# Attention block with a query tile's two passes run together at the start: key tiles in turn, two open banks of sums

## The chip, the cores and the metric

One core of a Trainium2 chip runs the whole kernel. The metric is device time in microseconds (us) of one execution. Five engines work side by side, each through its own list of instructions in order: TensorE (PE, matrix products), VectorE (DVE), ScalarE (ACT, here above all the exponentials), GpSimd (POOL) and SyncE (SP, which issues the DMAs). An instruction that has to wait holds up all that stands behind it on its engine. Matrix products land in PSUM, eight banks of 128 x 512 fp32.

## What is computed

A transformer block over 2048 tokens of width 640: layer norm, attention with 32 heads of 20 that share one key and one value head, residual; then layer norm, a gated GELU feed-forward of width 1536, residual.

```
q = (ln(x) @ wq)  as 32 heads of 20;   k = ln(x) @ wk;   v = ln(x) @ wv
p = softmax(q k^T / sqrt(20));   h = x + (p v, heads joined) @ wo
out = h + (gelu(ln(h) @ w_gate) * (ln(h) @ w_up)) @ w_down
```

The large part is the softmax: 32 x 2048 x 2048 exponentials.

## The kernel before

**Blocks, quads, passes.** The queries are cut into 16 tiles of 128 tokens, the keys too. A *pass* `(t, h)` is half `h` (16 heads, as 4 groups of 4) of query tile `t`: 32 passes in all. A *unit* or block is 128 keys x 512 (4 heads x 128 queries); the four blocks `hl` of a key tile in a pass make a *quad*. A pass has 16 quads, 64 blocks.

**Two ways to an exponential.** Most blocks go to ScalarE: `qk` (L873) writes scores to a bank, the exponential (L973) writes probabilities to `pbuf`, and PE multiplies by `v_ext` (L1087). ScalarE's blocks come in *cycles* of five: three blocks in banks 0 to 2 (an instruction of 128x1536) and two in banks 3 and 4 (128x1024). The last few key tiles of each pass go to VectorE instead (`stream_d`): it makes the exponential from the bits of an integer (L927, one instruction a block) and two shifted copies (L938, two a quad), which PE adds with weights `v_w`. `D_QUADS` gives the number of such key tiles by pass, `D_AHEAD` and `D_BEFORE_END` the cycles among which they are spread, and where `D_IN_SET` is 1 some cycles (places 1, 2, 4 and 6 of a pass) keep two blocks in the first set and leave its third bank to VectorE.

**Banks.** 0 to 2 and 3 to 4 hold scores. Bank 6 (`PVB`, `PV_pool`) holds the open sum of a pass, one pass at a time. Banks 5 and 7 (`AUX_pool`, `aux()`) are the side banks: projections, PE transposes, feed-forward, and the blocks for VectorE.

**Order.** Every engine's order is made ahead of the run by a planner (`_Sched`). Tasks carry dependences, priorities, an expected duration and slots of pools; it plays through them and writes the engines' lists with the semaphore waits. PE has three sources: the stream of score groups in fixed order (`sc.stream`), each with a margin (`spare`, from `MARGIN` and `MARGIN_2`); the sums (`Units`), which take as many finished quads as fit; and the rest. `PATIENCE`, `LAG` and `URGENT` are digits by pass or tile that shift these choices. The chip itself only sees the lists.

**The start.** SP loads x and the first half of wq (L578). Token tile by token tile, VectorE and GpSimd do the layer norm (L621 to L644), the tile is transposed (tile 0, and those in `T_CUT`, by PE, L667; the others by a DMA, L653), PE projects k and v (`kv_proj`, L701 and L703), and VectorE evicts them to `kT4` and `v_ext` (L712, L717). `q_first` projects the first half of query tile 0's q, enough for pass (0,0). The second half of wq is loaded once tile 9 is normalised, and `q_half(0, 1, ...)` with its DMA transpose `q_dma` (L747) makes the second half of q after that, for pass (0,1):

```
units += [(t, h, kt, hl) for kt in range(NT - n) for hl in range(4)]
if t == 9:
    dma_wq.append(load("sp", wq_sb[:, :, D // 2:D], ..., "wq1", 4.0, [ln1_nm[t]]))
...
q_half(0, 1, tk0, after_=[ln1_nm[Q_AFTER[0]]])
q_dma(0, tk0, 4)
```

**The rest.** When the last block of a pass is placed, `pv_open` opens its sum. When the sum is closed, `normalise` transposes it (L1106), divides and passes it on (L1113); then come `wo_proj`, a layer norm and `ffn`, interleaved with the next passes. The last tile is done by `last_tile` once the exponentials are over.

Of the kernel before, what the change touches and what calls it, by code (L numbers as in the profile page):

```python
# [45 lines left out]
class _Sched:  # L46
# [7 lines left out]

    PATIENCE = "42444444444444444442444443444444"
    WINDOW, ACTIVE, GAP = 3.42, 1.45, 0.25
# [48 lines left out]
    def schedule(self):  # L105
# [120 lines left out]
        while left:  # L226
            best = None
# [73 lines left out]
            if isinstance(t, int):  # L301
                t = self.units.take(at, t)
                for s in t.acq:
                    s.index = min(s.pool.open_for(s))
                    s.pool.busy[s.index] = True
                    t.extra += s.pool.users[s.index]
                    s.pool.users[s.index] = []
            else:
                ready[e] = [c for c in ready[e] if c[1] is not t]
                for s in t.acq:  # L310
                    p = s.pool
                    i = min(p.open_for(s), key=lambda i: (p.free_at[i], i))
# [105 lines left out]
def bass_sequential_preLN__grouped_kv_mqa__glu_gated_geglu__prompt_kernel(  # L418
# [93 lines left out]
    def bank(b):  # L512
        return ps[:, b * 512:(b + 1) * 512]
# [46 lines left out]

    LAG = "5333333333335533"
    T_CUT = {1: 5}
    KV_POOL = ()
# [20 lines left out]
    x_ready[2] = x_ready[3] = load("sp", xh[:, 2:4, :], x_view[:, 2:4, :], "x2", 4.9)  # L584
    dma_wq = [load("sp", wq_sb[:, :, 0:D // 2], wq_view[:, :, 0:D // 2], "wq0", 6.3)]
    for a in (4, 8):
        d = load("sp", xh[:, a:a + 4, :], x_view[:, a:a + 4, :], f"x{a}", 4.2 + a if a == 4 else 10.2)
        for t in range(a, a + 4):
            x_ready[t] = d
# [218 lines left out]
    def d_units(t, h):  # L808
        return 4 * int(D_QUADS[2 * t + h])

    D_QUADS = "04454544444444445444444444453533"
    D_AHEAD = "32222222222225222222222124223222"
    D_BEFORE_END = "33333333333333233331334233343233"
    MARGIN = "03333333233335333112333220613330"
    MARGIN_2 = "56666666666666366662666666343662"
    D_IN_SET = "11111111111111111111111111111111"

# [3 lines left out]
    units, d_kts, quads = [], {}, {}  # L821
    for t, h in passes:
        n = d_units(t, h) // 4
        quads[(t, h)] = [(len(units) + 4 * kt, kt) for kt in range(NT - n)]
        units += [(t, h, kt, hl) for kt in range(NT - n) for hl in range(4)]
        d_kts[(t, h)] = list(range(NT - n, NT))
    INSET = (1, 2, 4, 6)
# [16 lines left out]
    for p in passes:  # L844
        left = 4 * d_kts[p]
        if not left:
            continue
        for n in in_set:
            if cycles[n][0][0][:2] == p:
                d_of[(n, 2)] = p  # L850
                left = left[:-1]
        i = passes.index(p)
        n0, n1 = max(0, in_pass[p][0] - int(D_AHEAD[i])), in_pass[p][-1] - int(D_BEFORE_END[i])
        own = [(n, 1) for n in range(n0, n1 + 1) if (n, 1) not in d_of and len(cycles[n][1]) == 2]
        more = len(left) - len(own)
# [88 lines left out]
    def stream(n):  # L944
# [38 lines left out]
        for p in passes:  # L983
            if n == in_pass[p][-1]:
                pv_open(p)
# [14 lines left out]
    def pv_open(p):  # L1000

        t, h = p
        sl = state["pv"] = PV_pool.slot()
        for u, kt in quads[p]:
# [7 lines left out]
        end.opens = False  # L1012
        pending.append((p, sl, end))
        normalise(t, h, sl, end)

    class Units:


        def __init__(self):
            self.begun = False  # L1020

        def lists(self):
            p, sl, end = pending[0]
            return p, sl, end, owed[p], d_terms[p]

        @staticmethod
        def when(deps):
            return max(d.end + sc.HOP[d.eng] if d.end is not None else 1e9 for d in deps)

        def look(self, now):  # L1030

            if not pending:
                return None, 0
            p, sl, end, mine, terms = self.lists()
            base = 0.0
            if not self.begun:
                if sl.pool.busy[0]:
                    return None, 0
                base = sl.pool.free_at[0]
            at = [max(base, self.when(x[0])) for x in mine[:12]] + [max(base, self.when(x[0])) for x in terms]  # L1040
            at = [x for x in at if x < 1e8]
            if not at:
                return None, 0
            return min(at), sum(x <= now + 0.02 for x in at)

        def urgent(self):
            p, sl, end, mine, terms = self.lists()
            n = len([x for x in mine[:12] if self.when(x[0]) < 1e8])
            return n >= int(URGENT[sc.phase]) or p == passes[-1] or not any(
                x for x in mine if self.when(x[0]) > 1e8)  # L1050

        def take(self, now, n):
            p, sl, end, mine, terms = self.lists()
            got = []
# [6 lines left out]
            assert got  # L1061
            first = not self.begun
            last = not mine and not terms and not d_owed[p]
            t = end if last else sc.add("pe", None, 0.0, [], name=f"pv_{p}", cfg="col")
            t.deps = [d for x in got for d in x[0]]
            if first:
                t.acq = [sl]
                t.opens = lambda: bank(PVB)
            if last:
                t.opens = False  # L1070
                pending.pop(0)
            self.begun = not last
            for x in got:
# [4 lines left out]
            def fn(e):  # L1078
                ins = None
                for i, x in enumerate(got):  # L1080
# [17 lines left out]

    def normalise(t, h, pv_sl, pv_t):
# [325 lines left out]
    q_evicted[(0, 2)] = ln1_nm[Q_AFTER[1]]  # L1425
# [194 lines left out]
```

## Time and profile before

| | |
|---|---|
| time, median of 3 runs | 767.12 us (766.24 to 769.23) |
| the profiled execution's own time | 767.44 us |
| its span, first to last instruction | 765.8 us |
| PE busy | 722.0 us (94%) |
| DVE busy | 687.4 us (90%) |
| ACT busy | 732.5 us (96%) |
| L973, the exponentials on ACT | 667 instructions, 706.4 us |
| first exponential starts | 10.16 us |
| mean granted TensorE clock | 0.993 |

How to read it: the span is cut from one execution of the program; 1.6 us of that execution's time lie outside it. "Busy" is the time in which an engine ran at least one instruction. A line such as L973 is the line of the kernel before; in the changed kernel the same statements stand some lines lower. Rows of a timeline give the start, the length of the merged piece, the engine, the line, output <- input, the count, and in brackets the idle time ahead of it with what ended it.

### The profile page before, as it was taken

To read this page: it belongs to the slowest core of one execution; us is meant where nothing else is said; L and a number is where in the kernel's file an instruction comes from. 1 tells how busy PE (TensorE), PEld (TensorE's weight loads), DVE (VectorE), ACT (ScalarE), POOL (GpSimd) and SP (SyncE) were. 2 spreads that over 40 slices of the span, in tenths; PEclk is the share of its full clock that TensorE was granted. 3 is DMA by queue.
4 is the path that set the end of the run, shared out by engine and by line. 5 is a ranking of instruction groups with operands and counts; after the bars stand their busy time and mean duration, and the time that the engine had idled before them with its cause. 6 is when DMAs were issued, how large, how long until landed. Compare 5 with 4: busy or idle time off the path is not lost.

```text
span 765.8 us, 23888 instructions
## 1 busy us (share of the span) xinstructions
PE 722.0 (94%) x10693; PEld 264.3 (35%) x10693; DVE 687.4 (90%) x1275; ACT 732.5 (96%) x702; POOL 111.7 (15%) x185
## 2 busy tenths in 40 slices
PE   7898899999999999999999999999999999999987
PEld 3432233333333333333233333333333332333346
DVE  7777999999999999888999999999999999899862
ACT  5899999999999999999999999999999999999961
POOL 5410112001011111111101011021102101112100
PEclk9899999999999999999999999999999999999999
DMA  6692001020200303020001202102101200201201
GB/s 169 144 358 46 1 19 24 2 45 20 45 19 13 43 10 45 20 45 19 10 16 39 45 20 45 19 11 43 34 19 24 45 20 1 40 10 31 43 11 42
DMA packets 80604, 31.66 MB, mean 41 GB/s; under 512 B 71536, under 2 KB 79216, under 8 KB 80496
## 3 DMA queue, kind: packets, MB, share of 16 engines
q1 hardware_dynamic: 79184, 30.03, 18.1%
q8 instruction: 85, 1.39, 0.8%
q10 hardware_dynamic: 1312, 0.05, 0.1%
q14 instruction: 23, 0.19, 0.1%
HBM read 10.21 MB, written 2.62 MB: 17 GB/s over the span
## 4 chain that ended last, share of the span: by engine, by line
ACT 81%; PE 14%; DVE 3%; DMA 1%; issue 0%; SPq 0%; POOL 0%
ACT pbuf L973 78%; PE ps L533 5%; PE ps L873 4%; PE ps L1087 3%; ACT g_z L1241 2%; PE ps L1356 1%; DVE dbuf L927 1%; DMA wq_sb<-in_A_wq_dram 1%; DMA xnT<-xn_tmp 0%; PE ps L1365 0%; DVE g_gs L1226 0%; PE ps L701 0%; DVE stats L623 0%; SPq L578 0%; DVE stats L621 0%
## 5 line engine op out<-in xcount | busy, mean ns | idle before, releaser
L973 ACT ACTIVATE pbuf<-ps 128x1024 bf16<-128x1024 f32 (+1 forms) x667 | 706.4, 1267 | 5.1 <-PE ps L873 4.7
L927 DVE TENSOR_SCALAR dbuf<-ps 128x512 int16<-128x512 f32 x504 | 333.4, 684 | 33.2 <-PE ps L873 30.0
L873 PE MATMUL ps<-qT,kT 32*128 32x512 bf16 x2048 | 285.7, 386 | 27.3 <-ACT pbuf L973 21.8
L938 DVE TENSOR_SCALAR dbuf<-dbuf 128x2048 int16<-128x2048 int16 x252 | 168.4, 689 | 0.9
L873 PEld LDWEIGHTS ps<-qT,kT 32*128 32x128 bf16 x2048 | 74.0, 91 | 270.3 <-ACT pbuf L973 225.1
L1087 PE MATMUL ps<-pbuf,v_ext 128*32 128x512 bf16 (+3 forms) x2084 | 147.2, 331 | 0.6 <-ACT pbuf L973 0.4
L1087 PE MATMUL ps<-dbuf,v_w 128*32 128x512 bf16 x1512 | 132.2, 382 | 2.0 <-DVE dbuf L938 1.2
L1228 POOL TENSOR_TENSOR g_z<-g_gs 128x512 bf16<-128x512 bf16 x45 | 51.0, 1133 | 271.8 <-DVE g_gs L1226 271.8
L533 PE MATMUL ps<-wu_sb,xnT 128*32 128x512 bf16 x900 | 68.1, 383 | 1.8 <-DVE g_gs L1226 1.0
L1087 PEld LDWEIGHTS ps<-pbuf,v_ext 128*32 128x32 bf16 x2084 | 44.6, 94 | 67.9 <-issue 49.9
L533 PE MATMUL ps<-wd_sb,hhT 128*32 128x320 bf16 x1440 | 67.0, 301 | 0.0
L533 PE MATMUL ps<-wg_sb,xnT 128*32 128x512 bf16 x900 | 66.8, 382 | 0.1
L1087 PEld LDWEIGHTS ps<-dbuf,v_w 128*32 128x32 bf16 x1512 | 38.1, 95 | 37.6 <-issue 11.3
L1113 POOL TENSOR_TENSOR oN<-oT,rL 128x320 bf16<-128x320 f32 x30 | 22.5, 751 | 179.9 <-DVE rL L1108 156.6
L533 PEld LDWEIGHTS ps<-wd_sb,hhT 128*32 128x32 bf16 x1440 | 32.8, 96 | 23.7 <-issue 13.9
L533 PE MATMUL ps<-wq_sb,xnT 128*32 128x320 bf16 (+1 forms) x660 | 33.2, 298 | 1.0 <-DVE dbuf L927 0.4
L1234 DVE SCALAR_TENSOR_TENSOR g_us<-ps,g_gs 128x512 bf16<-128x512 f32 x45 | 30.6, 680 | 2.5 <-PE ps L533 2.4
L1226 DVE CAST g_gs<-ps 128x512 bf16<-128x512 f32 x45 | 30.7, 682 | 1.4 <-PE ps L533 1.1
L627 POOL CAST lnvb<-mv 128x1 bf16<-128x1 f32 x31 | 7.7, 248 | 166.7 <-DVE mv L625 166.5
L533 PE MATMUL ps<-wo_sb,onT 128*32 128x320 bf16 x600 | 31.1, 302 | 0.2 <-DVE dbuf L927 0.2
L533 PEld LDWEIGHTS ps<-wu_sb,xnT 128*32 128x32 bf16 x900 | 19.0, 95 | 26.6 <-issue 13.4
L533 PEld LDWEIGHTS ps<-wg_sb,xnT 128*32 128x32 bf16 x900 | 18.8, 95 | 23.8 <-issue 12.5
(96 smaller groups left out, 361.3 us busy)
## 6 DMA issues: line engine op xcount, KB each, us to landing
out_dram<-xh SPq DMA_DIRECT2D x15, 160.0 KB, 1.8
xh<-in_A_x_dram SPq DMA_DIRECT2D x3, 640.0 KB, 6.5
wg_sb<-in_B_w_gate_dram SPq DMA_DIRECT2D x1, 1920.0 KB, 10.6
wu_sb<-in_B_w_up_dram SPq DMA_DIRECT2D x1, 1920.0 KB, 15.1
wd_sb<-in_B_w_down_dram SPq DMA_DIRECT2D x1, 1920.0 KB, 19.7
wq_sb<-in_A_wq_dram SPq DMA_DIRECT2D x2, 400.0 KB, 4.5
wo_sb<-in_A_wo_dram SPq DMA_DIRECT2D x1, 800.0 KB, 4.8
xnT<-xn_tmp SPq DMA_TRANSPOSE x29, 2.6
```

The costliest lines, as they stand in the source:

```text
L533: ins = e.matmul(out[r, :], lhs[:, r], rhs, start=start, stop=stop, tile_position=(0, 32 * b))
L627: vb = add("pool", lambda e: e.tensor_copy(lnvb[:, ln.index:ln.index + 1], mv[:, ln.index, 1:2]), 0.2, [ag], name=f"{tag}vb_{t}")
L873: return e.matmul(bk.rearrange("p (g n) -> p g n", g=4), kT4[r, kt * P:(kt + 1) * P], qT[r, q_slot[t].index, 4 * h:4 * h + 4, :], start=Tr ...
L927: quad["bits"].append(sc.add("dve", lambda e: e.tensor_scalar(part(seg, w=slice(512 * item[0], 512 * item[0] + 512)), bk(), D_BIAS, 0.0, A ...
L938: dep = [sc.add("dve", lambda e, j=j, s=s: e.tensor_scalar(part(s), part(seg), D_SHIFT[j], None, ALU.add), 0.615, bits, prio=0.55 * HOT + ...
L973: exps.append(sc.add("act", lambda e, w0=w0, w1=w1, to=to: e.activation(pbuf[:, to:to + w1 - w0], ps[:, w0:w1], ACT.Exp, scale=EXP_SCALE), ...
L1087: ins = e.matmul(ps[32 * b:32 * b + 32, PVB * 512 + a:PVB * 512 + a + n].rearrange("p (a n) -> p a n", n=32), x[2], span.rearrange("p (a n ...
L1113: onorm[(t, h)] = c = sc.add(by, lambda e: e.tensor_tensor(oN[:, otk.index, h * (D // 2):(h + 1) * (D // 2)].rearrange("p (g l d) -> p l g ...
L1226: ge = sc.add("dve", lambda e, col=col, bk=bk: e.tensor_copy(g_gs[:, gsl.index, col], bk()), d_ps(512), [gm], prio=EVAC + pr, rel=[ax], na ...
L1228: sqt = sc.add("pool", lambda e, col=col: e.tensor_tensor(g_z[:, gsl.index, col], g_gs[:, gsl.index, col], g_gs[:, gsl.index, col], ALU.mult),
L1234: uts.append(sc.add("dve", lambda e, col=col, bk=bk: e.scalar_tensor_tensor(g_us[:, gsl.index, col], bk(), 0.5, g_gs[:, gsl.index, col], A ...
L1241: th = sc.add("act", lambda e: e.activation(g_z[:, gsl.index, :], g_z[:, gsl.index, :], ACT.Tanh, scale=GELU_C), d_act(1536), [zt], prio=- ...
```

## The change

Passes (0,0) and (0,1) of query tile 0 are no longer one after the other. The string `ORDER` takes their quads in turn, A for (0,0) and B for (0,1), each with its key tiles in order. The sum of (0,0) is now kept in a side bank and that of (0,1) in bank 6, both open at once, and `Units` takes quads of whichever has some ready first. The second half of wq is loaded right behind the first, ahead of x's tiles 4 to 11, and q's second half is made right after key tile 1's layer norm instead of after key tile 12's. Token tile 2 is transposed by PE as tile 1 is. VectorE gets 2 key tiles of pass (0,1) (8 blocks) where it had 4, spread from cycle 12 (`D_KEYS`) on, and 5 instead of 4 of pass (3,1); no cycle of the first two passes leaves its third bank to VectorE. Several digits of the planner's strings differ.

```
-    PATIENCE = "42444444444444444442444443444444"
+    PATIENCE = "42444444544444434442444343444444"
...
             if isinstance(t, int):
                 t = self.units.take(at, t)
                 for s in t.acq:
-                    s.index = min(s.pool.open_for(s))
+                    s.index = min(s.pool.open_for(s), key=lambda i: (s.pool.free_at[i], i))
                     s.pool.busy[s.index] = True
+                    s.pool.holder[s.index] = t
...
-    LAG = "5333333333335533"
-    T_CUT = {1: 5}
+    LAG = "5333333333335531"
+    T_CUT = {1: 5, 2: 5}
...
     dma_wq = [load("sp", wq_sb[:, :, 0:D // 2], wq_view[:, :, 0:D // 2], "wq0", 6.3)]
+    dma_wq.append(load("sp", wq_sb[:, :, D // 2:D], wq_view[:, :, D // 2:D], "wq1", 7.7))
     for a in (4, 8):
-        d = load("sp", xh[:, a:a + 4, :], x_view[:, a:a + 4, :], f"x{a}", 4.2 + a if a == 4 else 10.2)
+        d = load("sp", xh[:, a:a + 4, :], x_view[:, a:a + 4, :], f"x{a}", 9.6 if a == 4 else 11.6)
...
-    D_QUADS = "04454544444444445444444444453533"
-    D_AHEAD = "32222222222225222222222124223222"
-    D_BEFORE_END = "33333333333333233331334233343233"
-    MARGIN = "03333333233335333112333220613330"
-    MARGIN_2 = "56666666666666366662666666343662"
-    D_IN_SET = "11111111111111111111111111111111"
+    D_QUADS = "02454545444444445444444444453533"
+    D_AHEAD = "32222222222225222222222224225222"
+    D_BEFORE_END = "34333333313333233331334233343233"
+    MARGIN = "03333333033335332112313620613331"
+    MARGIN_2 = "52666666576666266662656766343668"
+    D_IN_SET = "00111111111111111111111111111111"
+    D_KEYS = 12
...
-    for t, h in passes:
-        n = d_units(t, h) // 4
-        quads[(t, h)] = [(len(units) + 4 * kt, kt) for kt in range(NT - n)]
-        units += [(t, h, kt, hl) for kt in range(NT - n) for hl in range(4)]
-        d_kts[(t, h)] = list(range(NT - n, NT))
+    for p in passes:
+        n = d_units(*p) // 4
+        d_kts[p], quads[p] = list(range(NT - n, NT)), []
+    ORDER = "AABABABBAAABABAABAABABAABABBBBBB"
+    together = [passes["AB".index(c)] for c in ORDER] + NT * passes[0:1] + NT * passes[1:2]
+    for p in together + [p for p in passes[2:] for _ in range(NT)]:
+        kt = len(quads[p])
+        if kt < NT - len(d_kts[p]):
+            quads[p].append((len(units), kt))
+            units += [p + (kt, hl) for hl in range(4)]
...
         n0, n1 = max(0, in_pass[p][0] - int(D_AHEAD[i])), in_pass[p][-1] - int(D_BEFORE_END[i])
+        if i < 2:
+            n0 = D_KEYS
...
-            if n == in_pass[p][-1]:
+            if n == max(in_pass[p][-1], in_pass[passes[0]][-1]):
                 pv_open(p)
...
-        sl = state["pv"] = PV_pool.slot()
+        if p == passes[0]:
+            sl, bk = aux()
+        else:
+            sl, bk = pvb()
...
     class Units:
         def lists(self):
-            p, sl, end = pending[0]
-            return p, sl, end, owed[p], d_terms[p]
+            return [x + (owed[x[0]], d_terms[x[0]]) for x in pending[:2 if pending[0][0] == passes[0] else 1]]
...
+        def best(self):
...
             if last:
-                t.opens = False
-                pending.pop(0)
-            self.begun = not last
+                pending[:] = [x for x in pending if x[0] != p]
+                other = [self.begun[x[0]] for x in pending if x[0] in self.begun]
+                t.opens = other[0] if other else False
...
-                                ps[32 * b:32 * b + 32, PVB * 512 + a:PVB * 512 + a + n].rearrange("p (a n) -> p a n", n=32),
+                                bk()[32 * b:32 * b + 32, a:a + n].rearrange("p (a n) -> p a n", n=32),
...
-        a = sc.add("dve", lambda e: e.transpose(oT[:, sl.index, :], bank(PVB)), 0.63, [pv_t], prio=pr,
+        a = sc.add("dve", lambda e: e.transpose(oT[:, sl.index, :], bk()), 0.63, [pv_t], prio=pr,
...
-        if t == 9:
-            dma_wq.append(load("sp", wq_sb[:, :, D // 2:D], wq_view[:, :, D // 2:D], "wq1", 4.0, [ln1_nm[t]]))
         kv_proj(t)
-    q_half(0, 1, tk0, after_=[ln1_nm[Q_AFTER[0]]])
-    q_dma(0, tk0, 4)
+        if t == 1:
+            q_half(0, 1, tk0)
+            q_dma(0, tk0, 4)
```

More of the change, by code (lines that the diff above doesn't have):

```diff
@@ L1012, in pv_open @@
         end.opens = False
-        pending.append((p, sl, end))
-        normalise(t, h, sl, end)
+        pending.append((p, sl, end, bk))
+        normalise(t, h, sl, end, bk)
     class Units:
         def __init__(self):
-            self.begun = False
+            self.begun = {}
         def lists(self):
-            p, sl, end = pending[0]
-            return p, sl, end, owed[p], d_terms[p]
+            return [x + (owed[x[0]], d_terms[x[0]]) for x in pending[:2 if pending[0][0] == passes[0] else 1]]
         @staticmethod
@@ L1028, in when @@
             return max(d.end + sc.HOP[d.eng] if d.end is not None else 1e9 for d in deps)
+        def best(self):
+            found = []
+            for entry in self.lists() if pending else []:
+                p, sl, end, bk, mine, terms = entry
+                base = 0.0
+                if p not in self.begun:
+                    open_ = sl.pool.open_for(sl)
+                    if not open_:
+                        continue
+                    base = min(sl.pool.free_at[i] for i in open_)
+                at = [max(base, self.when(x[0])) for x in mine[:12]] + [max(base, self.when(x[0])) for x in terms]
+                at = [x for x in at if x < 1e8]
+                if at:
+                    found.append((min(at), len(found), at, entry))
+            return min(found) if found else None
         def look(self, now):
-            if not pending:
+            found = self.best()
+            if found is None:
                 return None, 0
[L1034 to L1044, printed above, removed]
+            return found[0], sum(x <= now + 0.02 for x in found[2])
         def urgent(self):
-            p, sl, end, mine, terms = self.lists()
+            p, sl, end, bk, mine, terms = self.best()[3]
             n = len([x for x in mine[:12] if self.when(x[0]) < 1e8])
@@ L1052, in take @@
         def take(self, now, n):
-            p, sl, end, mine, terms = self.lists()
+            p, sl, end, bk, mine, terms = self.best()[3]
             got = []
@@ L1061, in take @@
             assert got
-            first = not self.begun
+            first = p not in self.begun
             last = not mine and not terms and not d_owed[p]
@@ L1067, in take @@
                 t.acq = [sl]
-                t.opens = lambda: bank(PVB)
+                t.opens = bk
+                self.begun[p] = bk
             if last:
-                t.opens = False
-                pending.pop(0)
-            self.begun = not last
+                pending[:] = [x for x in pending if x[0] != p]
+                other = [self.begun[x[0]] for x in pending if x[0] in self.begun]
+                t.opens = other[0] if other else False
             for x in got:
@@ L1097, in bass_sequential_preLN__grouped_kv_mqa__glu_gated_geglu__prompt_kernel, with normalise @@
     URGENT = "55555555555555555556555555555655"
-    def normalise(t, h, pv_sl, pv_t):
+    def normalise(t, h, pv_sl, pv_t, bk=lambda: bank(PVB)):
         sl = ON_pool.slot()
```

## The prediction

> **What bounds the kernel now.** I read the page first, for the busy shares and the chain that ended last.
>
> ```profile
> PE 722.0 (94%) x10693; PEld 264.3 (35%) x10693; DVE 687.4 (90%) x1275; ACT 732.5 (96%) x702; POOL 111.7 (15%) x185
> ACT 81%; PE 14%; DVE 3%; DMA 1%; issue 0%; SPq 0%; POOL 0%
> ```
>
> ScalarE (ACT) carries the chain. Its work is the exponentials, so I asked the view of stages for two stretches: from the first exponential to 26.5 us, and from there to the last one.
>
> ```profile
> core 0: us, PE busy (x) PEld busy (x) DVE busy (x) ACT busy (x) POOL busy (x), PEclk, DMA share, GB/s
> 10.16:26.50 16.34, 13.16 (x153) 6.23 (x145) 14.29 (x59) 12.32 (x11) 9.00 (x26) 0.79 0.58 122
> 26.50:736.80 710.30, 680.26 (x10124) 238.78 (x10122) 653.24 (x1166) 709.88 (x671) 95.59 (x135) 1.00 0.17 37
> ```
>
> After 26.5 us ScalarE is busy 709.88 of 710.30 us: 710 us of nothing but ScalarE. All that any reordering can win there is 0.4 us. Before it, ScalarE is idle 16.34 - 12.32 = 4.02 us. The timeline of ScalarE says where (idle time in front of each piece is in brackets):
>
> ```profile
> 10.16 1.45 ACT L973 ACTIVATE pbuf<-ps 128x1536 bf16<-128x1536 f32 x1 [0.68 <-PE ps L873]
> 12.28 2.37 ACT L973 ACTIVATE pbuf<-ps 128x1024 bf16<-128x1024 f32 x2 [0.67 <-PE ps L873]
> 15.46 1.02 ACT L973 ACTIVATE pbuf<-ps 128x1024 bf16<-128x1024 f32 x1 [0.81 <-PE ps L873]
> 16.74 2.37 ACT L973 ACTIVATE pbuf<-ps 128x1536 bf16<-128x1536 f32 x2 [0.26 <-PE ps L873]
> 19.76 1.45 ACT L973 ACTIVATE pbuf<-ps 128x1536 bf16<-128x1536 f32 x1 [0.66 <-PE ps L873]
> 21.62 2.37 ACT L973 ACTIVATE pbuf<-ps 128x1024 bf16<-128x1024 f32 x2 [0.41 <-PE ps L873]
> 25.20 45.67 ACT L973 ACTIVATE pbuf<-ps 128x1024 bf16<-128x1024 f32 x42 [1.21 <-PE ps L873]
> ```
>
> Six holes behind the first exponential: 0.67 + 0.81 + 0.26 + 0.66 + 0.41 + 1.21 = 4.02 us. In each ScalarE waits for scores, because pass (0,0) has one key tile, four blocks, per tile that the layer norm delivers. This is the whole stake of putting two passes together: 4.02 us of 767.
>
> **The price in ScalarE work.** The digits of D_QUADS sum to 126 before and 125 after: pass (0,1) gives VectorE 2 key tiles instead of 4, pass (3,1) 5 instead of 4. So 4 blocks of 128x512 move to ScalarE (1544 to 1548). Both kernels have 667 exponentials; listed, 457 of two blocks and 210 of three become 453 and 214. Their durations in the gapless stretch:
>
> ```profile
> L973 ACT ACTIVATE pbuf<-ps 128x1024 bf16<-128x1024 f32 x453 | 461.7, 1136 | 1.4 <-PE ps L873 1.2
> L973 ACT ACTIVATE pbuf<-ps 128x1536 bf16<-128x1536 f32 x205 | 319.0, 1556 | 0.2
> ```
>
> One block more costs 1556 - 1136 = 420 ns, four cost 1.68 us. Nothing covers it: it lies on the engine that is the chain. So the most that the change can give is 4.02 - 1.68 = 2.34 us, 0.3%, by every hole closing.
>
> **Which holes close.** I walk the new order with these rows.
>
> ```profile
> 2.11 5.18 DMA wq_sb<-in_A_wq_dram
> 2.63 1.07 SPq L578 DMA_DIRECT2D xh<-in_A_x_dram  x2
> xh<-in_A_x_dram SPq DMA_DIRECT2D x1, 640.0 KB, 6.5
> 8.88 0.44 PE L667 MATMUL ps<-ident,xn_tmp 128*128 128x128 bf16 x5
> 9.72 0.39 PE L873 MATMUL ps<-qT,kT 32*128 32x512 bf16 x3 [0.40 <-DVE qT L803]
> 10.12 0.47 DVE L621 BATCH_NORM_STATS2 stats<-xh 128x6 f32<-128x320 bf16 x1
> 10.59 0.45 PE L701 MATMUL ps<-xnT,wk 128*128 128x128 bf16 x5
> 11.51 0.27 DVE L712 TENSOR_SCALAR kT<-ps 128x128 bf16<-128x128 f32 x1
> 11.70 0.17 DVE L717 CAST v_ext<-ps 128x20 bf16<-128x20 f32 x1
> 65.81 0.86 PE L533 MATMUL ps<-wq_sb,xnT 128*32 128x320 bf16 x20
> 34.41 0.49 DVE L743 CAST q_tok<-ps 128x320 bf16<-128x320 f32 x1
> qT<-q_tok SPq DMA_TRANSPOSE x1, 2.5
> 14.53 3.42 DMA xnT<-xn_tmp
> ```
>
> *First exponential.* The changed PE order has the first 4 of the 20 matmuls of q's second half ahead of the first scores, waiting for wq's second half. wq's first half lands at 2.11 + 5.18 = 7.29 us. Behind it the first four-tile load of x (issued at 2.63) lands at 9.1: 640 KB in 1.8 us, so 400 KB take some 1.1 us and the second half lands near 8.4 (estimate). PE comes there at 9.3, when the transposition of 8.88 is done, and has until 9.72. Cost 0; at worst, if it landed only where x does with the 1.1 us added, 10.2, the scores start some 0.7 us late. The loads of x move back by the same 1.1 us: the bn_stats of 10.12, which reads that load, may wait 0.1 to 0.2, and q's eviction, next behind it on VectorE, has to wait for PE until 10.8 anyway.
>
> *Hole 1* (key tile 1). PE does the other 16 matmuls (0.86 x 16/20 = 0.7) after the scores: 9.72 + 0.39 + 0.7 = 10.8, and the key projection of tile 1 comes then instead of at 10.59. On VectorE q's eviction (0.49) takes the place of a bn_stats ahead of kT. PE also does tile 2's transposition (0.44) ahead of the next scores. So this hole doesn't close: 0.67 becomes between 0.67 and 0.67 + 0.2 + 0.44 = 1.3; I take 0.85, since the transposition only partly outlasts kT's eviction.
>
> *Holes 2 to 6.* After hole 1 ScalarE has 8 blocks of pass (0,0), until 12.3 + 0.2 + 2.4 = 14.9, and then wants key tile 0 of pass (0,1). Its q is evicted from 10.9 to 11.4, its transposing DMA takes 2.5 (the same one in the kernel before) to 3.42 (a tile's, at 14.53): 13.9 to 14.8; scores to exponential are 10.16 - 9.72 = 0.44, so it comes at 14.3 to 15.3. Hole 0 to 0.4. From there ORDER asks for key tiles 2, 3, 4 at quads 5, 7, 10 in place of 3, 4, 5 of pass (0,0): a quad is 4 blocks, 1.95 us at 5 blocks in 1.45 + 1.02, so tile 4 is due near 27 us where it was due by 18. Holes 2 to 6 were all before 25.2 with a tile wanted each 1.95 us; now two passes share each tile. I take 0.3 us for what is left of them, between 0 and their whole 3.35.
>
> *VectorE.* A key tile there is 4 conversions and 2 shifts:
>
> ```profile
> L927 DVE TENSOR_SCALAR dbuf<-ps 128x512 int16<-128x512 f32 x504 | 333.4, 684 | 33.2 <-PE ps L873 30.0
> L938 DVE TENSOR_SCALAR dbuf<-dbuf 128x2048 int16<-128x2048 int16 x252 | 168.4, 689 | 0.9
> 120.00:160.00 40.00, 37.81 (x512) 12.15 (x514) 38.93 (x69) 39.91 (x38) 7.28 (x9) 1.00 0.11 20
> 160.00:200.00 40.00, 38.62 (x603) 14.13 (x591) 38.50 (x69) 40.00 (x40) 3.48 (x6) 1.00 0.12 26
> 200.00:240.00 40.00, 39.22 (x602) 13.71 (x605) 36.28 (x65) 40.00 (x39) 5.25 (x8) 1.00 0.10 21
> ```
>
> 4 x 0.684 + 2 x 0.689 = 4.11 us. Passes 0 and 1 lose two, 8.2 us of work that was under ScalarE's and so gives nothing by itself. Pass (3,1) gets one more. By its cycles (74 to 83 of the 334 that the code makes) it lies at 171 to 193 us, where VectorE is busy 38.50 of 40: with 4.11 that is 42.6, over by 2.6 us. The next stretch has 3.7 us free, and pass (2,1), which has 5 key tiles already, lies in 120 to 160 with ScalarE idle only 0.09 us. I take 0, at worst 2.6.
>
> *Two open banks.* Pass (0,0) sums into one of the two side banks, so projections, q, and VectorE's blocks share the other until about 60 us. Cover: ScalarE has at least one exponential (0.9 to 1.45 us) in hand while PE waits for an eviction (0.27 + 0.17 for a key tile). I take 0; the bound is with the rivals.
>
> *Digits.* PATIENCE, LAG, the margins: they reorder PE by fractions of a us under a gapless ScalarE, and the listed order of the last tile on ScalarE is the same. 0.
>
> **Sum.** Saved 4.02 - 0.85 - 0.3 = 2.87; added 1.68; net -1.19 us. On the profiled execution's own 767.44 that is 766.25. The median shown is 767.12, 0.32 below that execution, so I forecast **765.9 us**, -0.16%. A measurement of this kernel can tell some 0.5%, 3.84 us, from no change.
>
> **The clock, row and rule.**
>
> ```profile
> 15.00:20.00 5.00, 3.17 (x38) 1.60 (x34) 4.31 (x18) 3.62 (x4) 2.54 (x8) 0.82 0.52 103
> 20.00:25.00 5.00, 5.00 (x52) 2.73 (x48) 3.74 (x18) 3.58 (x3) 2.54 (x8) 0.50 0.67 176
> 22.06 0.71 PE L701 MATMUL ps<-xnT,wk 128*128 128x128 bf16 x5
> ```
>
> TensorE has a thin stretch at 15 to 20 (3.17 of 5 busy) and then a granted clock of 0.50 until 25; a key projection then takes 0.71 instead of 0.45, and three of the holes (0.66, 0.41, 1.21) lie there. If the halving came again in the new order at the same length, those 2.28 us could return: 765.9 + 2.28 - 0.3 = 767.9. [...]
>
> **Rivals.** *The holes move (0.20).* The change doesn't do what it says: q's second half comes late (3.42 or more), and each PE wait for a transposed tile, now placed ahead of more score groups, opens a hole of the old kind; or the clock halves as above; or pass (3,1) overruns. For it: at 14.53 a tile took 3.42 us to land and everything waited. Against: the due times fall back by up to 9 us. Holes of 2.8 to 4.0 us in all: 767 to 768.8.
>
> *One side bank (0.11, slower).* From 13 us on, 13 key tiles, 4 q halves and VectorE's blocks go through one bank, and PE, which takes its work in order, stands at each until VectorE has evicted the one before; the score groups are queued behind. If each of the 13 adds its 0.44 us of eviction to ScalarE's path, that is 5.7 us: 765.9 + 5.7 = 771.6. It decides once VectorE comes to the eviction later than the exponential in hand lasts (0.9 us). For it: VectorE was busy 14.29 of 16.34 us there. Against: ORDER spreads the 16 tiles over 26 quads of 1.95 us, 3.2 us each, in place of 1.95.
>
> *Every hole but the first closes and something unpriced helps (0.03, faster by over 0.5%).* The terms end at 767.12 - 2.34 = 764.8; 763.3 needs more than they hold.
>
> **Numbers.** Forecast 0.66, with its own range 764.8 to 767; with the moved holes 0.86 is within 0.5%. Faster 0.03, same 0.86, slower 0.11. The range for 8 in 10 runs from 764.4 (all holes closed, and the 0.3 between execution and median) to 769.0 (the moved holes with the same).
>
> **What would show it.** Right: ScalarE idle in 10 to 30 us falls from 4.02 to some 1.2 us, with the first hole the largest; from there gapless to the last exponential; the last exponential ends about 1.2 us earlier; granted clock near 1 in 20 to 25. Wrong: exponentials waiting on scores between 14 and 60 us, with PE waiting for VectorE's kT or q_tok (side bank) or for a DMA (late tile); a first exponential later than 10.2; ScalarE idle at 170 to 200 (overrun of VectorE).

## The result: 4,225 us, by a second program that the change switched on

The changed kernel takes 4,224.89 us (median of 4 runs, 4,220.46 to 4,228.92). The kernel before took 767.84 us beside it (4 runs, 766.24 to 769.23). The ratio is 5.498, 95% interval 5.484 to 5.513. The profiled execution took 4,221.93 us, with a span of 4,220.6. The forecast was 765.9.

The page of the changed kernel shows another kernel than the one that was predicted. First its heads, then its chain:

```profile
span 4220.6 us, 106308 instructions
PE 2302.1 (55%) x50182; PEld 930.3 (22%) x50182; DVE 2167.8 (51%) x2792; ACT 1766.2 (42%) x1231; POOL 216.7 (5%) x359
...
ACT  9999999233232323232323232322323232232322
...
PEclk9999999655555555555555555555555555555555
...
ACT 36%; DVE 32%; PE 28%; DMA 2%; issue 1%; POOL 1%; POOLq 0%; SPq 0%
...
L1553 DVE TENSOR_REDUCE mx<-ps 128x1 f32<-128x2048 f32 x512 | 1173.2, 2291 | 1707.3 <-PE ps L1549 1707.3
L1557 ACT ACTIVATE pbuf<-ps,mx 128x2048 bf16<-128x2048 f32 x512 | 1007.4, 1967 | 2299.4 <-DVE mx L1555 2299.4
L1549 PE MATMUL ps<-kT,qT 32*128 32x512 bf16 x2048 | 927.3, 602 | 1718.7 <-ACT pbuf L1557 1718.7
L983 ACT ACTIVATE pbuf<-ps 128x1024 bf16<-128x1024 f32 (+1 forms) x667 | 709.0, 1287 | 4.2 <-PE ps L883 3.6
```

PE has 50,182 matmuls, where the kernel before has 10,693. In the 40 slices ScalarE is full for seven, some 740 us, and then at two or three tenths to the end. The groups name the rest: the 667 exponentials of L983 are all there, with 4.2 us of idle time, and beside them 512 maxima over whole rows of scores (L1553), 512 exponentials of 128x2048 (L1557) and 2,048 matmuls of scores (L1549). 512 is 16 query tiles x 32 heads: all of the attention once more, a head at a time. ScalarE's timeline shows the seam (the busy time of a row follows its start):

```profile
756.27 0.44 ACT L1419 ACTIVATE xh<-ps 128x320 bf16<-128x320 f32 x1 [2.15 <-PE ps L1385]
761.88 1.28 ACT L1557 ACT_TABLE_LOAD   x1 [5.17 <-PEq L1497]
785.97 1.97 ACT L1557 ACTIVATE pbuf<-ps,mx 128x2048 bf16<-128x2048 f32 x1 [22.81 <-DVE mx L1555]
```

At 761.88 us, near the end of the kernel before (765.8), ScalarE loads its table for L1557. What runs from there stands in the code, in a part that the diff doesn't touch. The exponentials of the program up to here have no maximum subtracted. So `check_sums` (L1167) takes the reciprocals `rL` of all sums and asks whether each lies between 2^-64 and 2^80; `raise_flag` (L1180) sums the answers over the 128 partitions, and every engine branches on that number (P is 128):

```
e.br_eq(good, P, on_true="all_done", on_false="with_maximum").branch_hint(hints[e.engine])   # L1526
```

`with_maximum` (L1527) is a second program, which makes everything again with each row's maximum subtracted. In the kernel before the number is 128 and the program ends. In the changed one it isn't. The second program's chain is serial; these are six pieces of it, in order of time:

```profile
787.99 1.90 PE ps L1549 x4
789.91 2.29 DVE mx L1553
792.27 0.13 DVE mx L1555
792.43 1.98 ACT pbuf L1557
794.45 1.90 PE ps L1549 x4
796.37 2.29 DVE mx L1553
```

Scores, maximum, its negative, exponential, and again scores: 794.45 - 787.99 = 6.46 us a head, as all four banks of scores are held until the exponential has read them (PE's wait for L1557 comes to 1718.7 us in the groups). 512 x 6.46 = 3,308 us, nearly the whole of the 3,457 by which the kernel is late.

**Why the sums are out of range: a name.** The change gives `normalise` a parameter for the bank of the sums, and a function that reads it later:

```
def normalise(t, h, pv_sl, pv_t, bk=lambda: bank(PVB)):                               # L1119
    a = sc.add("dve", lambda e: e.transpose(oT[:, sl.index, :], bk()), 0.63, ...)     # L1126
    ...
    else:
        ax, bk = aux()                                                                # L1148
```

The lambda of L1126 runs when the planned program is written out, long after `normalise` has returned. It then finds what `bk` was last set to. In 31 passes that is the parameter. The `else` branch runs in one pass alone, the second half of the last query tile, and there L1148 sets `bk` to the side bank into which PE transposes that half's result. So, by the code, the last pass's sums are transposed from the side bank, and the reciprocals made from them are not all within the bounds. That is the theory (A in the texts below). Its rival (B) is that the two open banks of sums spoil each other.

### The profile page after: what moved, and what is told of

Same layout as the page of the kernel before. It is cut to its first block, busy times and chain, and to the rows that moved or that the text cites. A ratio compares the mean times of both kernels' runs of the same rounds, so it can differ in the third digit from the quotient of the medians.

```text
span 4220.6 us, 106308 instructions
## 1 busy us (share of the span) xinstructions
PE 2302.1 (55%) x50182; PEld 930.3 (22%) x50182; DVE 2167.8 (51%) x2792; ACT 1766.2 (42%) x1231; POOL 216.7 (5%) x359
## 4 chain that ended last, share of the span: by engine, by line
ACT 36%; DVE 32%; PE 28%; DMA 2%; issue 1%; POOL 1%; POOLq 0%; SPq 0%
DVE mx L1553 27%; ACT pbuf L1557 21%; PE ps L1549 21%; ACT pbuf L983 14%; PE ps L534 5%; DVE mx L1555 2%; DMA hhT<-g_us 1%; PE ps L883 1%; ACT g_z L1261 1%; PE ps L1107 1%; DVE g_us L1254 1%; DMA xnT<-xn_tmp 0%; DVE g_us L1266 0%; DVE g_z L1259 0%; POOL g_z L1248 0%
## 5 line engine op out<-in xcount | busy, mean ns | idle before, releaser
L1553 DVE TENSOR_REDUCE mx<-ps 128x1 f32<-128x2048 f32 x512 | 1173.2, 2291 | 1707.3 <-PE ps L1549 1707.3
L1557 ACT ACTIVATE pbuf<-ps,mx 128x2048 bf16<-128x2048 f32 x512 | 1007.4, 1967 | 2299.4 <-DVE mx L1555 2299.4
L1549 PE MATMUL ps<-kT,qT 32*128 32x512 bf16 x2048 | 927.3, 602 | 1718.7 <-ACT pbuf L1557 1718.7
L983 ACT ACTIVATE pbuf<-ps 128x1024 bf16<-128x1024 f32 (+1 forms) x667 | 709.0, 1287 | 4.2 <-PE ps L883 3.6
L1549 PEld LDWEIGHTS ps<-kT,qT 32*128 32x128 bf16 x2048 | 208.6, 123 | 2087.5 <-ACT pbuf L1557 1807.2
L1570 PEld LDWEIGHTS ps<-dbuf,v_ext 128*32 128x32 bf16 x32768 | 318.4, 102 | 413.1 <-issue 343.9
L1570 PE MATMUL ps<-dbuf,v_ext 128*32 128x32 bf16 x32768 | 361.9, 192 | 46.5 <-DMA dbuf<-pbuf 45.1
L534 PE MATMUL ps<-wg_sb,xnT 128*32 128x512 bf16 x1860 | 148.9, 437 | 41.8 <-DMA xnT<-xn_tmp 23.2
L534 PE MATMUL ps<-wd_sb,hhT 128*32 128x320 bf16 x2976 | 151.2, 348 | 33.9 <-DMA hhT<-g_us 33.1
L534 PE MATMUL ps<-wu_sb,xnT 128*32 128x512 bf16 x1860 | 147.5, 430 | 1.5 <-DVE dbuf L937 0.8
L1248 POOL TENSOR_TENSOR g_z<-g_gs 128x512 bf16<-128x512 bf16 x93 | 100.5, 1080 | 548.4 <-DVE g_gs L1246 548.4
L1261 ACT ACTIVATE g_z<-g_z 128x1536 bf16<-128x1536 bf16 x31 | 47.8, 1541 | 116.3 <-DVE g_z L1259 116.3
```

Source lines behind the costliest of these rows:

```text
L534: ins = e.matmul(out[r, :], lhs[:, r], rhs, start=start, stop=stop, tile_position=(0, 32 * b))
L983: exps.append(sc.add("act", lambda e, w0=w0, w1=w1, to=to: e.activation(pbuf[:, to:to + w1 - w0], ps[:, w0:w1], ACT.Exp, scale=EXP_SCALE), ...
L1248: sqt = sc.add("pool", lambda e, col=col: e.tensor_tensor(g_z[:, gsl.index, col], g_gs[:, gsl.index, col], g_gs[:, gsl.index, col], ALU.mult),
L1261: th = sc.add("act", lambda e: e.activation(g_z[:, gsl.index, :], g_z[:, gsl.index, :], ACT.Tanh, scale=GELU_C), d_act(1536), [zt], prio=- ...
L1549: ins = e.matmul(bank(kb), qT[r, q_sl.index, g, :], kT4[r, kb * 512:kb * 512 + 512], start=True, stop=True, tile_position=(32 * hl, 0))
L1553: m = sc.add("dve", lambda e: e.tensor_reduce(mx[:, m_sl.index, 0:1], ps[:, 0:S], mybir.AxisListType.X, ALU.max), 2.2, [a], prio=pr, acq=[ ...
```

## The experiments

**The name alone, taken away.** In the changed kernel, two lines of `normalise`:

```
-            ax, bk = aux()
-            view = lambda: bk().bitcast(BF16)[:, 0:3 * P]
+            ax, tb = aux()
+            view = lambda: tb().bitcast(BF16)[:, 0:3 * P]
```

> The changed kernel with one local name altered: in the last branch of normalise the side bank is called tb, so that bk keeps meaning the bank handed in as the new parameter. Theory A (the assignment in that branch takes over the name bk, the transposition of the sums of the last pass reads the side bank, the flag isn't 128, and the second program runs): no second program; the last exponential stays near 738.4 us and the time near 767 us (766 to 769). Rival B (two open banks of sums in passes 0 and 1 give sums that are out of range): nothing altered, some 4,222 us with the exponentials of L1557 in the trace. Of the reordered start by itself, under A: 767.4 if the last tile again has TensorE at its full clock, up to 769 if it is halved there as in the kernel before.

768.77 us (12 runs), the kernel before 768.73 beside it (23 runs): ratio 0.9996, 95% interval 0.9964 to 1.0028. No L1557 is left in the trace. The two banks of sums are open in this kernel too, so the rival falls.

**The name alone, put in.** In the kernel before:

```
-    def normalise(t, h, pv_sl, pv_t):
+    def normalise(t, h, pv_sl, pv_t, bk=lambda: bank(PVB)):
...
-        a = sc.add("dve", lambda e: e.transpose(oT[:, sl.index, :], bank(PVB)), ...
+        a = sc.add("dve", lambda e: e.transpose(oT[:, sl.index, :], bk()), ...
```

> The kernel before, with nothing of the change but the parameter bk of normalise and the transposition that reads bk(): one bank of sums, the old order, the old digits. Theory A: the last pass reads the side bank and the second program runs, 767 + 3,460 = 4,225 us. Rival B (it takes two open banks): 767 us.

4,226.16 us (one run). Its groups, beside those of the changed kernel above, are the same second program behind the old order:

```profile
L1534 DVE TENSOR_REDUCE mx<-ps 128x1 f32<-128x2048 f32 x512 | 1173.4, 2292 | 1706.9 <-PE ps L1530 1706.9
L1538 ACT ACTIVATE pbuf<-ps,mx 128x2048 bf16<-128x2048 f32 x512 | 1007.1, 1967 | 2303.3 <-DVE mx L1536 2303.3
```

So the name is both enough and needed. That it spoils the last pass's sums and no others is read from the code; no run showed the sums one by one.

**The price of the second program.** In the kernel before, `R_MIN, R_MAX = 2.0 ** 80, 2.0 ** 80`.

> The kernel before with the bound R_MIN of the check of sums raised from 2^-64 to 2^80: no sum meets it and the branch always takes the second program. It prices that program by itself: if it is all that the change added, 767 + 3,457 = 4,224 us within 10. If something of the new order makes the second program slower too, less than 4,200.

4,224.87 us (one run), inside the 4,220.46 to 4,228.92 of the changed kernel. The second program is all that the change added of any size.

**The changed first program by itself.** In the changed kernel, `on_false="all_done"`: both ways of the branch lead to the end. This leaves out the second program, and with it the right result for half of the last query tile's heads.

> The changed kernel, whose branch on the flag goes to the end in both cases: the second program is left out, and with it the right result for the second half of the heads of the last query tile under theory A. It times the first program as the change left it. A and B both: 767 to 769 us, as e1_renamed within 0.5 us. Rival C (part of the time is lost in the first program, which runs slower when the other is to follow): over 775.

766.16 us (10 runs), ratio 0.9955 to the kernel before, interval 0.9925 to 0.9986. That is under what each theory said, by more than the 0.5 us allowed, though its profiled execution (768.0 us of span) was no faster. The last rows of VectorE and the end of the span show where it comes from. The kernel before, then e1_renamed, then this one:

```profile
span 765.8 us, 23888 instructions
...
q14 instruction: 23, 0.19, 0.1%
...
760.33 0.49 DVE L1261 TENSOR_TENSOR xh<-xh,ps 128x320 bf16<-128x320 bf16 x1 [1.14 <-PE ps L533]
```

```profile
span 767.2 us, 23755 instructions
...
761.93 0.49 DVE L1281 TENSOR_TENSOR xh<-xh,ps 128x320 bf16<-128x320 bf16 x1 [1.14 <-PE ps L534]
```

```profile
span 768.0 us, 23750 instructions
...
q14 instruction: 17, 0.14, 0.1%
...
765.71 0.49 DVE L1281 TENSOR_TENSOR xh<-xh,ps 128x320 bf16<-128x320 bf16 x1 [1.14 <-PE ps L534]
```

From the end of VectorE's last instruction to the end of the span it is 4.98 us, 4.78 us, and here 1.80. In a kernel that can branch, the second program stands between the branch and the end in the code (L1527 to L1603), and the way to the end is a jump over it; here there is no other way than to the end.

**The same in the kernel before.** `on_false="all_done"` there:

> The kernel before whose branch goes to the end in both cases; the second program is left out of it. In e3_after_no_second, which also lacks it, the span ended 1.8 us after VectorE's last instruction, in the kernel before 5.0 and in e1_renamed 4.8. If that is the jump over the second program (its target has to be fetched): 3 us less than before at the same clock, 765.7, and the span ends 1.8 us after VectorE's last instruction here too. If it is something of e3 alone: as before, 768.7. The difference to e3_after_no_second at the same clock is then the worth of the new start alone, which e1_renamed gave as 0.7 us.

766.21 us (12 runs; 769.67 for the kernel before beside it), ratio 0.9957, interval 0.9931 to 0.9983, and the same end:

```profile
span 764.8 us, 23883 instructions
...
762.46 0.49 DVE L1261 TENSOR_TENSOR xh<-xh,ps 128x320 bf16<-128x320 bf16 x1 [1.14 <-PE ps L533]
```

1.85 us. Queue q14, which the page lists as one for instructions, differs in time as well: from 755 to 770 us it brings eight packets in the kernel before, all behind VectorE's last instruction and some past the end of the span, eight in e1_renamed, and none in e3_after_no_second. So a run that skips the second program pays for it as well, with or without the change.

**What is left: the start.** Single executions of e1_renamed spread from 765 to 776 us, those of the kernel before from 766 to 775, and most of that goes with the granted clock of TensorE. A least-squares fit of the span on the clock, with one slope and a constant for each kernel, over the 156 executions of the kernels in this table (80 of the kernel before, 76 of the others; residual 0.74 us) gives 4.2 us more for each 0.01 less clock, and at full clock these spans (standard errors 0.2 to 0.4). It is a line through the runs, and doesn't show by itself that the clock is the cause:

| kernel | span at full clock, us | against the kernel before | granted clock, median | time, median, us |
|---|---|---|---|---|
| before | 762.4 | | 0.989 | 768.2 to 769.7, by set of runs |
| e1_renamed | 761.8 | -0.6 | 0.986 | 768.77 |
| g1_before_no_second | 760.0 | -2.4 | 0.989 | 766.21 |
| e3_after_no_second | 759.3 | -3.1 | 0.987 | 766.16 |
| h1_old_digits | 775.3 | +12.9 | 0.980 | 784.88 |
| h2_free_fill | 764.4 | +2.0 | 0.993 | 769.41 |
| h3_free_fill_all | 765.1 | +2.7 | 0.994 | 769.29 |
| h5_fill_late | 762.6 | +0.2 | 0.994 | 766.28 |

The new start is worth -0.6 us between the two kernels that can branch and -0.7 between the two that can't, with standard errors of 0.2 and 0.3. (The second two ran in different sets; between these sets the kernel before, fitted set by set, differs by 0.2.) The jump is worth 2.4 in both orders. The experiments below asked what became of the rest of the 1.19 us that the prediction had.

**Four blocks fewer on ScalarE.** e1_renamed with `D_QUADS = "03454545..."` for `"02454545..."`.

> e1_renamed with one more key tile of pass (0,1) on VectorE (digit 3 for 2): 1,540 to 1,544 blocks on ScalarE instead of 1,548, as the kernel before had them. The prediction priced 4 blocks at 1.68 us. If that price holds: 1.7 us less than e1_renamed at the same granted clock, 767.1 for 768.8. If VectorE, which these 4 blocks need at 10 to 60 us, becomes late for the evictions of keys, q and values: no gain, or up to 2 us more.

788.14 us (6 runs), ratio 1.0243 (1.0198 to 1.0287): neither. ScalarE's exponentials end at 738.6 us, near where they did. The loss is behind that:

```profile
738.66 1.28 ACT L1343 ACT_TABLE_LOAD   x1
...
769.32 1.48 ACT L1261 ACTIVATE g_z<-g_z 128x1536 bf16<-128x1536 bf16 x1 [12.19 <-DVE g_z L1259]
```

L1261 belongs to the feed-forward layer of a whole query tile. In the kernel before the last of its kind starts at 745.82; here one starts at 746.90 and one more at 769.32. The edit at the start made the planner plan everything behind it anew, and its plan leaves a tile's layer over for the end. So this run doesn't price 4 blocks.

**The digits.** That is what the other digit strings in the diff are about:

> e1_renamed with the six digit strings that the change altered beside D_QUADS (PATIENCE, LAG, D_AHEAD, D_BEFORE_END, MARGIN, MARGIN_2) put back to those of the kernel before. The prediction priced these digits at 0: then 768.8 as e1_renamed. f2a and f1_filled, where the plan was made anew behind a small edit at the start, took some 20 us more, lost near the end; if the digits are what fits the rest of the plan to its start, this kernel loses 10 to 25 us in the same place: 780 to 795.

784.88 us (6 runs), ratio 1.0222 (1.0188 to 1.0257), the loss in the same place: the last L1261 starts at 763.70 after 5.39 us of idle time. The prediction priced these digits at 0. They are worth 775.3 - 761.8 = 13.5 us: they fit the rest of the plan to the new start, and without them the change would have been slower even with its name mended.

**The clock at the start.** e1_renamed lost its clock there. Its stages (busy us of PE, PEld, DVE, ACT, POOL, then granted clock, DMA share, GB/s):

```profile
10.00:20.00 10.00, 8.16 (x112) 3.81 (x109) 9.26 (x37) 8.80 (x8) 5.58 (x18) 1.00 0.46 98
20.00:30.00 10.00, 10.00 (x91) 4.42 (x88) 8.30 (x33) 9.39 (x9) 5.00 (x13) 0.53 0.93 153
30.00:40.00 10.00, 10.00 (x88) 4.67 (x89) 4.96 (x23) 8.63 (x8) 3.11 (x9) 0.50 0.38 72
40.00:50.00 10.00, 9.62 (x125) 3.79 (x122) 2.40 (x8) 8.72 (x9) 0.00 (x0) 0.78 0.99 370
```

At half clock PE is shown busy all of 20 us, and each hole of ScalarE from 20 to 46 us ends on PE's scores; ScalarE loses 0.61 + 1.37 + 1.28 us from 20 to 50 us. Filler matmuls, which the planner already uses, might keep the clock up (theory F, a guess made from these rows). The first try let the planner put in more of them (`return 2.2 if at < 70.0 else self.ACTIVE` for the constant 1.45), in the renamed kernel and in the kernel before:

> e1_renamed, where up to 70 us the planner puts in filler matmuls (zeros, into a bank in use) whenever PE's planned activity in 3.42 us falls below 2.2 us instead of 1.45: 336 filler matmuls in all for 180. Theory F (the halved clock of 20 to 42 us comes from a PE that is too thin before it): the granted clock rises from some 0.987 towards 1.00 and, at 4.1 us for 0.01 (the slope over the runs of e1_renamed's call), the time falls by 3 to 5 us to some 764. Rival G (the clock falls whatever PE does at the start; in e3_after_no_second it fell at 49 us behind a stretch with 8.4 of 10 us busy): clock and time as e1_renamed, 768 to 769, or later by the fillers on the path.

> The kernel before with the same rule for fillers up to 70 us: 344 filler matmuls for 208. Theory F: clock from some 0.988 to 0.995 or more, 3 us less than before, 765.7. Rival G: as before, 768.7.

790.89 us (ratio 1.0287, 1.0259 to 1.0315) and 794.69 (1.034, 1.031 to 1.037): the plan made anew costs 20 us here too, and the times tell nothing of F or G. Nor did the clock over the whole run rise as F has it: medians of 0.989 and 0.986, with 0.987 in the kernel before beside them. In both profiled executions it was 0.97 from 10 to 60 us (0.76 in e1_renamed, 0.93 in the kernel before), and most of the time was lost at the end: from the last exponential to the end of the span it is 44.4 and 51.5 us, for 28.9 in the kernel before. So the next ones leave every engine's order as it is and write the fillers into the plan's idle places, up to 70 us and up to 735:

```
+            if e == "pe" and opened is not None and at < 70.0 and t.__class__ is not int and t.cfg == "row" and (
+                    at - free[e] >= 0.25 and ...):
+                for _ in range(int((at - free[e]) / 0.25)):
+                    f = self.add("pe", lambda eng, o=opened: self.filler[0](eng, o), 0.0, ..., name="extra", cfg="col")
+                    ...
```

> e1_renamed with the order of every engine as it was, and up to 70 us more filler matmuls written into PE's order at the places where the plan has PE idle for 0.25 us or more: 264 for 180. f1_filled, with the plan made anew, can't tell what the fillers do to the clock's price. Theory F (thin PE at the start brings the halved clock): granted clock 0.992 or more and, at 4.2 us for 0.01, some 2 to 3 us less than e1_renamed, 766. Rival G (the clock falls whatever PE does): clock as e1_renamed, time 768.8, or up to 2 us more by 84 matmuls that come late.

> As h2_free_fill, but up to 735 us: 544 filler matmuls for 180. e3_after_no_second had its clock halved at 140 to 150 us and lower at 200 to 210, so that not all of the loss is at the start. Theory F: clock 0.995 or more, 765. Rival G: clock as e1_renamed, and the fillers lengthen PE's queue in a stretch where it is busy 94 to 97 of 100 us: up to 10 us more.

769.41 and 769.29 us (12 runs each), ratios 1.0008 (0.9990 to 1.0027) and 1.0008 (0.9989 to 1.0027). The granted clock rose nearly as F says, from a median of 0.986 to 0.993 and 0.994, with the lowest of 12 runs at 0.990 and 0.992 where e1_renamed's was 0.968 (the kernel before had 0.989 and 0.990 beside them). The time did not fall: at equal clock the two kernels are 2.0 and 2.7 us behind the kernel before. PE and ScalarE in h2_free_fill:

```profile
20.59 0.53 PE L709 MATMUL ps<-xnT,wk 128*128 128x128 bf16 x5 [2.18 <-DMA xnT<-xn_tmp]
21.84 1.45 ACT L989 ACTIVATE pbuf<-ps 128x1536 bf16<-128x1536 f32 x1 [1.62 <-PE ps L889]
```

PE waits 2.18 us for a transposed tile of x whose DMA took 5.06 us, against 3.52 for the same tile in e1_renamed and a wait of 0.65, and ScalarE stands 1.62 us behind it. In h3_free_fill_all that DMA took 5.63, PE waited 2.8 and ScalarE 2.38. Leaving out the fillers ahead of that wait (`25.0 < at < 70.0`):

> h2_free_fill without the fillers that it wrote in ahead of 25 us: 240 filler matmuls for the 180 of e1_renamed. h2_free_fill raised the clock and lost the gain, its largest piece in a wait of 2.2 us at 18 to 21 us for a transposed tile of x. If the fillers ahead of that wait cause it: no such wait (0.7 us or less), clock near 0.990, time 766 to 767.5, ahead of both kernels. If each filler costs its own time on PE's path: 768 to 769 as e1_renamed, with a higher clock and later work.

766.28 us (12 runs; 768.37 for the kernel before beside it, 17 runs), ratio 0.9979, interval 0.9953 to 1.0004. The wait is 0.64 again, and the median of the clock is 0.994. This is the lowest median here of a kernel that keeps the second program, 2.1 us under the one before, but the interval still holds no change; at equal clock the fit has it 0.2 us behind. How the fillers on PE made this DMA take longer stays open.

## Why the prediction was wrong, and what of it held

**The step that failed** is in "Two open banks" and in the list of rivals. The prediction priced the second bank as traffic on the other side bank, at 0, and its rival "the change doesn't do what it says" was about holes that stay open. Neither asked which bank `normalise` reads in the last pass, though L1126 is in the diff, and neither priced the branch on the sums, although the kernel holds a whole second program behind it. What the runs showed in place of that 0 is 3,457 us: the second program, set off by one name (4,226.16 with the name alone, 768.77 with all of the change but the name). In the profile of before that program has no row, so its price had to be bounded: 512 heads with scores, a maximum and an exponential in series. The range of 764.4 to 769.0 was that of a kernel that runs one program, and nothing in it stood for the other.

**The terms of the sum, on a kernel that runs one program.** h5_fill_late's profiled execution had a granted clock of 1.00 throughout, so its ScalarE shows them undisturbed:

```profile
9.95 1.45 ACT L989 ACTIVATE pbuf<-ps 128x1536 bf16<-128x1536 f32 x1 [0.68 <-PE ps L889]
12.33 15.93 ACT L989 ACTIVATE pbuf<-ps 128x1024 bf16<-128x1024 f32 x14 [0.93 <-PE ps L889]
28.50 110.70 ACT L989 ACTIVATE pbuf<-ps 128x1024 bf16<-128x1024 f32 x103 [0.24 <-PE ps L889]
253.55 31.07 ACT L989 ACTIVATE pbuf<-ps 128x1024 bf16<-128x1024 f32 x29 [0.39 <-PE ps L889]
```

And the same of the changed kernel itself, up to its first long stretch without a hole, its clock at 0.50 from 20 to 30 us:

```profile
10.08 1.45 ACT L983 ACTIVATE pbuf<-ps 128x1536 bf16<-128x1536 f32 x1 [0.68 <-PE ps L883]
12.46 7.80 ACT L983 ACTIVATE pbuf<-ps 128x1024 bf16<-128x1024 f32 x7 [0.93 <-PE ps L883]
20.53 1.45 ACT L983 ACTIVATE pbuf<-ps 128x1536 bf16<-128x1536 f32 x1 [0.27 <-PE ps L883]
22.40 5.87 ACT L983 ACTIVATE pbuf<-ps 128x1024 bf16<-128x1024 f32 x5 [0.41 <-PE ps L883]
28.73 4.77 ACT L983 ACTIVATE pbuf<-ps 128x1536 bf16<-128x1536 f32 x4 [0.47 <-PE ps L883]
33.97 107.42 ACT L983 ACTIVATE pbuf<-ps 128x1536 bf16<-128x1536 f32 x100 [0.47 <-PE ps L883]
```

- *First exponential*, cost 0: right. 10.08 here and 9.95 there, for 10.16 before; in e1_renamed 10.27.
- *Hole 1*, 0.85 taken between 0.67 and 1.3: 0.93 in both, and in e1_renamed.
- *Holes 2 to 6*, 0.3 taken: 0.24 at full clock, right. With the clock halved 0.27 + 0.41 + 0.47 + 0.47 = 1.62 in the changed kernel. That is the clock's halving that the prediction set beside its sum, with up to 2.28 us. That the sum stands without it was the author's estimate: no run shows that the new order by itself keeps the clock up, and from 20 to 30 us it was 0.50 in the changed kernel, 0.53 in e1_renamed and 1.00 in e3_after_no_second. The halving was sized too small, and as a thing of the start alone: in e1_renamed these holes are 0.47 + 0.47 + 0.82 + 0.41 + 0.27 + 0.60 = 3.04 us, and in e3_after_no_second, whose clock stood at 1.00 until it fell near 49 us, five holes between 52 and 66 us come to 4.27.
- *Four blocks*, 1.68 us: the exponentials of h5_fill_late take 707.9 us, 1.5 more than the 706.4 of before; in the changed kernel 709.0, 2.6 more. The size fits, but roughly: g1_before_no_second has the exponentials of the kernel before and takes 707.2. Why the same instructions take some 1 us more in some executions isn't settled.
- *VectorE at (3,1)*, 0: right, no hole of ScalarE at 171 to 193 us in either kernel. The 0.39 at 253.55 wasn't foreseen.
- *One side bank*: no hole between 34 and 250 us in these two, so 0 was right, and this rival is out.
- *Digits*, 0: wrong by 13.5 us as a price of the part. That the whole comes out the same is luck of the forecast: start and digits were changed together, and nothing in the prediction says that they had to be.
- *The sum*, -1.19 us: -0.6 and -0.7 at equal clock, with standard errors of 0.2 and 0.3: the sign right, about half of the size. The sign that the prediction named, a last exponential that ends 1.2 us earlier, shows where the clock stayed up: 735.9 us in h5_fill_late, for 736.9 before, but 738.4 in the changed kernel and 740.1 in e1_renamed. By the fit, the clock of each run, at 4.2 us for 0.01, outweighs the gain.
- *Readings that are off and leave the sum as it is*: by `ORDER`, key tiles 2, 3 and 4 are first wanted at quads 4, 6 and 9, not 5, 7 and 10; 1.45 + 1.02 us for 5 blocks make 1.98 us a quad, not 1.95; and holes of 2.8 us would give 767.6, not 767.

So the reading of the start held in the main, and the forecast of a time that can't be told from that of the kernel before is what the kernel gives once a name is mended. It was wrong about the kernel as it stands, because a part of the program that had never run was left out of the sum.

## What to carry to other kernels

A kernel with a guard has two programs. Ask of each edit whether it touches what the guard reads, and put the price of the other path, from its own loop, among the rivals with a chance of its own. In code that builds a program from functions called later, a name that such a function reads belongs to the whole enclosing function: a parameter added above may be taken over by an assignment below, so search for all of them (or bind it, `lambda e, bk=bk: ...`). And where a planner makes the order, an edit at the start is priced together with the retuning behind it; to test one part, leave the order fixed.

## What of the hardware was not expected

**The jump to the end.** A branch that skips the second program costs 2.4 us by the fit, and leaves 4.35 us (h5_fill_late), 4.78 (e1_renamed) and 4.98 (the kernel before) behind VectorE's last instruction, for 1.80 and 1.85 without it. The queue q14 carries 23 packets of instructions in the kernel before and 17 in e3_after_no_second. The traces show the gap, and q14's packets in it or right behind it; no run showed that the chain waits for them.

**A busy PE that stays at half clock.** In e1_renamed PE is shown busy 10.00 of 10 us from 20 to 40 us, and the granted clock is 0.53 and 0.50 there. A stretch of PE that the profile shows as full did not keep the clock up by itself; from 10 to 60 us PE is busy 43.92 of 50 us in h5_fill_late at clock 1.00, and 46.39 in e1_renamed at 0.76:

```profile
10.00:60.00 50.00, 43.92 (x594) 18.41 (x586) 32.84 (x111) 48.76 (x43) 15.37 (x41) 1.00 0.79 210
```

More fillers raised the median over 12 runs from 0.986 to 0.993 and 0.994, also where those added stood behind 25 us of the plan (h5_fill_late). Where some stood ahead of the wait for a transposed tile the time did not fall.
